# Attention scores from unpadded queries on quarters of the array, and another loading order at the start

## The chip, the cores and the metric

The kernel runs on one core of a Trainium2 chip. The metric is the device time of one execution, in microseconds (us). The engines are named as in the profile: PE is the matmul engine (TensorE) and PEld its weight loads, DVE is VectorE, ACT is ScalarE, POOL is GpSimd, and SP is the engine on which all the DMAs of this kernel are issued. They run side by side and wait for one another at semaphores; each takes its instructions in the order in which they stand.

## What is computed

Attention of 4 batches, 8 heads, 576 positions and head dimension 64, and then two feed-forward layers on the 2304 rows that come out:

```python
mask_local = (rel >= 0) & (rel < 32)                    # heads 0 to 3
mask_strided = (rel >= 0) & (pos_k % 32 == pos_q % 32)  # heads 4 to 7
x = softmax(where(mask, q @ k.T / 8, -1e9)) @ v         # then (2304, 512)
h = x @ w_in;  x = (h - tanh(h)) @ w_out                # d_ff = 2048
xn = x / sqrt(mean(x * x) + 1e-6) * rms_g
x = (silu(xn @ w_gate) * (xn @ w_val)) @ w_out          # d_ff = 1536
```

Activations are float32 and the weights float64. The kernel decodes the float64 words of a weight tile to a high and a low float32r part on ACT and DVE, and every product of the two layers is three matmuls (high by high, low by high, high by low).

## The kernel before

**Blocks and groups.** The rows are cut into nine blocks of 256: blocks 0 to 3 are the first 256 positions of the four batches, block 4 the last 64 positions of all four, blocks 5 to 8 the middle 256 positions. `groups = [(0, 1), (2, 3), (4,), (5, 6), (7, 8)]` pass through the first layer one after the other; the second layer follows on 512 rows at a time. In the first layer a unit `(g, f, a, e)` is group g, slice f of 16 of d_ff, and rows a to e: twelve matmuls `ps_h<-xs,w`, then tanh and a split on ACT and DVE, then twelve matmuls `ps_x<-g,w`. `xs` holds the attention output of the group, split into two parts.

**Attention of a block.** `Local` does heads 0 to 3 and `Dense` heads 4 to 7 (block 4 has `Strided` for these, on POOL and DVE). Each has two parts of three stages. `st_s` makes scores: `ps_s` on PE, then four fused mask-and-minimum reductions on DVE (`sm`, `nm`), four exponentials on ACT, and a division on DVE. `st_p` transposes `sm` on PE (`ps_p`) and copies it to `pT`. `st_v` multiplies by v (`ps_v`, tile `v` for Local and `vd` for Dense), and ACT (L353, L446) and DVE (L354, L447) write the two halves of the result to `xs`. So a block has four score stages, except block 4, which has two.

**Scores before.** The queries of two heads stand in one tile, `qz` or `qd`, that is padded with zeros off the diagonal, so that one matmul over all 128 rows and 128 columns of the array gives the scores of two heads: a stage is four such matmuls of 64, 96 or 128 columns (64 keys for Dense in blocks 0 to 3, 128 in blocks 5 to 8). The zeros come from memsets, and the queries from DMAs of 64 partitions, in pieces of 256 bytes. Each matmul of float32 shows as two in the trace, so a stage of four shows as x8. The stage takes one PSUM tile of the pool `ps_m` (block 0 takes `ps_m` and `ps_h` in turn), and each of these pools has two.

**What sets the order.** A string `START` writes out the beginning, letter by letter: `a` to `e` and `A` to `E` load blocks 0 and 1, `t` the table of masks, `w` a weight, `0` and `1` run the next stage of a block, `s` decodes one step, `U` runs a unit. Then a loop goes through the units; `st1.to` decodes weights ahead of it, and `pe_work` hands out the attention stages of the next group over the f. A scheduler then orders the instructions of each engine from the program's priorities and its own estimates of time; it may take a matmul from a later stage into an earlier place. A DMA on SP waits for the eighth one before it. Weights (`raw`, 512 KB) and the attention tiles of blocks 0 and 1 share the 32 buffers of pool `wts`.

```python
START = 'dt0AB0w00100ss100w1CDsbEU101w10csw1a1sw110w0Usw1s1e'
```

Of the kernel before, what the change touches and what calls it, by code (L numbers as in the profile page):

```python
# [17 lines left out]
BIG = 1.0e30  # L18
# [3 lines left out]
START = 'dt0AB0w00100ss100w1CDsbEU101w10csw1a1sw110w0Usw1s1e'  # L22
# [3 lines left out]
def attn_moe_moe_kernel(  # L26
# [54 lines left out]
    PR = 4 * 64  # L81
# [16 lines left out]
    tab = one.tile([128, 416], F32, name="tab")  # L98
    mask, ident = tab[:, 0:96], tab[:, 160:288]
    dmask = {64: tab[:, 96:160], 128: tab[:, 288:416]}  # L100
    qz = one.tile([128, 4, 2, 128], F32, name="qz")
# [108 lines left out]
    def copy(j, i):  # L210
        if j < EA and "aavaaaaa"[4 * j + i] == "v":
            return nc.vector.tensor_copy
        return nc.scalar.copy


    class Local:
# [9 lines left out]
        def load_qk(self):  # L226
            if self.j < EA:
                self.kT = wts.tile([128, 1024], F32, tag="w", name="kT")[:, :2 * self.kw]
                self.kT = self.kT.rearrange("r (p t) -> r p t", p=2)
                self.qz = wts.tile([128, 1024], F32, tag="w", name="qz").rearrange("r (u p t) -> r u p t", p=2, t=128)  # L230
                (nc.vector if self.j == 0 else nc.gpsimd).memset(self.qz[0:64, :, :, 64:128], 0.0)
                nc.gpsimd.memset(self.qz[64:128, :, :, 0:64], 0.0)
            else:
                self.kT = one.tile([128, 2, 4 * (W + 64)], F32, tag="kT", name="kT")[:, :, :self.kw]
                self.qz = qz
                if self.j == EA:
                    nc.gpsimd.memset(qz, 0.0)
            for b, t0, n, x0 in self.runs:
                for hh in range(2):
                    r = slice(64 * hh, 64 * hh + 64)  # L240
                    nc.sync.dma_start(  # L241
                        out=self.qz[r, x0 // 64:(x0 + n) // 64, :, r].rearrange("r u p t -> r (u p) t"),
                        in_=q_loc[b, r, t0 // 32:(t0 + n) // 32, :],
                    )
                o = self.at[x0 // 64]
                d = W if t0 == 0 else 0
                nc.sync.dma_start(out=self.kT[:, :, o + d:o + W + n], in_=k_loc[b, :, :, t0 - W + d:t0 + n])

        def load_v(self, i):
            us = list(self.units[i])  # L250
            self.v[i] = room(self.j, att, "v", tag="v")[0:96, :512].rearrange("k (u f) -> k u f", u=2)
            if self.wide(us[0]) == 64:
# [757 lines left out]
```

## Time and profile before

| what | us |
|---|---|
| median of 3 runs (lowest 945.73, highest 947.6) | 946.35 |
| the profiled execution | 946.1 |
| its span, from the first to the last instruction | 944.3 |
| PE busy in that span | 927.7 |
| DVE / ACT / POOL busy | 510.5 / 357.9 / 65.2 |

The profile is one execution, and its times count from the start of the span. PE is the engine to follow. A busy PE is not a PE at its peak: matmuls overlap, and each is recorded for longer than the next one has to wait, so the price of a group of matmuls is read as the distance from its start to the start of the next group. The granted clock (PEclk) is a share of 2.4 GHz.

### The profile page before, as it was taken

The numbers are of one execution on the slowest core, as the hardware profiler recorded it, in microseconds if no ns is written. First come the engines' busy times: TensorE is split into PE (matmuls) and PEld (weight loads), VectorE is DVE, ScalarE is ACT, GpSimd is POOL, SyncE is SP. The second block draws the span as 40 slices with busy tenths as digits, with TensorE's granted clock in tenths as the row PEclk, the third lists the DMA queues.
The fourth block names the chain that finished last, engine by engine and source line by source line (L and its number), as shares of the span: only waits on it lengthen the run. The fifth ranks groups of instructions, "written<-read, shape, count | busy, mean of one in ns | idle before, by whom it ended". The sixth has DMA issues, their size and how long they took to land.

```text
span 944.3 us, 13675 instructions
## 1 busy us (share of the span) xinstructions
PE 927.7 (98%) x5274; PEld 782.9 (83%) x5274; DVE 510.5 (54%) x1223; ACT 357.9 (38%) x838; POOL 65.2 (7%) x105
## 2 busy tenths in 40 slices
PE   6899999999999999999999999999999999999998
PEld 5788888888999888888888888888888888888897
DVE  4899998883554434249999783262125312421212
ACT  5776753322554443246656332222112211111211
POOL 2000035760000000000000000000000000000000
PEclk9799999999999999999999999999999999999999
DMA  9936334420321300065535201101010001000100
GB/s 210 336 123 216 117 84 133 110 81 1 111 68 62 89 32 1 1 220 180 162 113 196 76 37 44 45 1 45 1 44 1 23 1 45 0 1 1 45 1 23
DMA packets 51488, 72.66 MB, mean 77 GB/s; under 512 B 24928, under 2 KB 35552, under 8 KB 51424
## 3 DMA queue, kind: packets, MB, share of 16 engines
q1 hardware_dynamic: 51424, 71.80, 24.6%
q8 instruction: 41, 0.67, 0.3%
q14 instruction: 23, 0.19, 0.1%
HBM read 62.34 MB, written 9.44 MB: 76 GB/s over the span
## 4 chain that ended last, share of the span: by engine, by line
PE 94%; DVE 2%; DMA 1%; SPq 1%; issue 0%; ACT 0%
PE ps_x L111 37%; PE ps_h L111 37%; PE ps_m L111 16%; PE ps_s L111 2%; PE ps_v L111 2%; DMA raw<-in_w_in_dram 1%; PE ps_p L326 1%; PE ps_p L426 1%; DVE ct L142 0%; DVE ct L139 0%; SPq L241 0%; DVE w L151 0%; SPq L379 0%; DVE ct L138 0%; DVE sm L297 0%
## 5 line engine op out<-in xcount | busy, mean ns | idle before, releaser
L111 PE MATMUL ps_x<-g,w 128*128 128x512 f32 (+1 forms) x984 | 220.9, 368 | 0.0
L111 PE MATMUL ps_h<-xs,w 128*128 128x512 f32 (+1 forms) x984 | 220.2, 368 | 0.2 <-DVE tg L653 0.2
L111 PEld LDWEIGHTS ps_h<-xs,w 128*128 128x128 f32 x984 | 170.4, 191 | 29.2 <-DVE xs L354 0.4
L111 PEld LDWEIGHTS ps_x<-g,w 128*128 128x128 f32 x984 | 168.7, 188 | 29.5
L111 PE MATMUL ps_h<-xn,w 128*128 128x512 f32 (+1 forms) x720 | 159.0, 369 | 0.0
L111 PE MATMUL ps_m<-xn,w 128*128 128x512 f32 (+1 forms) x720 | 158.6, 368 | 0.0
L111 PE MATMUL ps_x<-w,p 128*128 128x512 f32 x648 | 157.9, 391 | 0.0
L765 DVE SCALAR_TENSOR_TENSOR s<-ps_m,s 128x512 f32<-128x512 f32 (+1 forms) x60 | 38.2, 637 | 219.1 <-PE ps_m L111 219.1
L111 PEld LDWEIGHTS ps_h<-xn,w 128*128 128x128 f32 x720 | 126.8, 188 | 24.4
L111 PEld LDWEIGHTS ps_m<-xn,w 128*128 128x128 f32 x720 | 126.0, 188 | 23.1
L111 PEld LDWEIGHTS ps_x<-w,p 128*128 128x128 f32 x648 | 120.7, 188 | 25.6
L653 DVE SCALAR_TENSOR_TENSOR tg<-ps_h,tg 128x512 f32<-128x512 f32 (+1 forms) x82 | 51.0, 622 | 87.5 <-ACT tg L648 87.5
L764 ACT ACTIVATE s<-ps_h 128x512 f32<-128x512 f32 (+1 forms) x60 | 33.3, 556 | 159.4 <-PE ps_h L111 159.4
L648 ACT ACTIVATE tg<-ps_h 128x512 f32<-128x512 f32 (+1 forms) x82 | 44.5, 543 | 99.9 <-PE ps_h L111 96.5
L767 ACT CAST p<-s 128x512 fp32r<-128x512 f32 (+1 forms) x60 | 34.7, 578 | 121.1 <-DVE s L765 121.1
L659 ACT CAST g<-tg 128x512 fp32r<-128x512 f32 (+1 forms) x82 | 46.6, 569 | 49.5 <-DVE tg L653 49.3
L664 DVE TENSOR_TENSOR g<-tg,g 128x512 fp32r<-128x512 f32 (+1 forms) x82 | 53.4, 651 | 17.0 <-ACT g L659 16.6
L131 ACT ACTIVATE ca<-raw 128x512 f32<-128x512 f32 x68 | 45.7, 674 | 42.4 <-DVE ct L139 18.6
L768 DVE TENSOR_TENSOR p<-s,p 128x512 fp32r<-128x512 f32 (+1 forms) x60 | 38.2, 637 | 25.1 <-ACT p L767 24.9
L150 ACT CAST w<-ct 128x512 fp32r<-128x512 f32 x68 | 42.0, 620 | 16.8 <-DVE ct L142 16.7
L151 DVE TENSOR_TENSOR w<-ct,w 128x512 fp32r<-128x512 f32 x68 | 46.5, 689 | 3.0 <-ACT w L150 2.8
L139 DVE SCALAR_TENSOR_TENSOR ct<-ca,ct 128x512 uint32<-128x512 uint32 x68 | 46.6, 689 | 0.2
(87 smaller groups left out, 681.2 us busy)
## 6 DMA issues: line engine op xcount, KB each, us to landing
raw<-in_w_out_dram SPq DMA_DIRECT2D x28, 512.0 KB, 5.5
raw<-in_w_in_dram SPq DMA_DIRECT2D x16, 512.0 KB, 7.9
raw<-in_w_gate_dram SPq DMA_DIRECT2D x12, 512.0 KB, 3.7
raw<-in_w_val_dram SPq DMA_DIRECT2D x12, 512.0 KB, 3.7
x2d<-xe SPq DMA_DIRECT2D x36, 128.0 KB, 1.8
x<-x2d SPq DMA_DIRECT2D x16, 256.0 KB, 4.0
out_dram<-o SPq DMA_DIRECT2D x16, 256.0 KB, 2.0
v<-in_v_loc_dram SPq DMA_DIRECT2D x14, 192.0 KB, 2.6
```

The costliest lines, as they stand in the source:

```text
L111: nc.tensor.matmul(out_, lhsT, rhs, start=start, stop=stop, skip_group_check=True)
L131: nc.scalar.mul(out=a, in_=hi.bitcast(F32), mul=2.0 ** -111)
L139: nc.vector.scalar_tensor_tensor(out=t, in0=a, scalar=0x80000000, in1=t, op0=ALU.bitwise_and, op1=ALU.bitwise_or)
L150: nc.scalar.copy(out=t[:, 0], in_=self.b)
L151: lo_eng.tensor_tensor(out=t[:, 1], in0=self.b, in1=t[:, 0].bitcast(F32), op=ALU.subtract)
L648: nc.scalar.activation(out=t, in_=h_of[g, f, a], func=ACTF.Tanh, scale=WS)
L653: nc.vector.scalar_tensor_tensor(out=t, in0=h_of.pop((g, f, a)), scalar=WS, in1=t, op0=ALU.mult, op1=ALU.subtract)
L659: nc.scalar.copy(out=t[:, 0], in_=t_of[g, f, a])
L664: nc.vector.tensor_tensor(out=t[:, 1], in0=t_of.pop((g, f, a)), in1=t[:, 0].bitcast(F32), op=ALU.subtract)
L765: nc.vector.scalar_tensor_tensor(out=s, in0=r[1], scalar=WS, in1=s, op0=ALU.mult, op1=ALU.mult)
L767: nc.scalar.copy(out=t[:, 0], in_=s)
L768: nc.vector.tensor_tensor(out=t[:, 1], in0=s, in1=t[:, 0].bitcast(F32), op=ALU.subtract)
```

## The change

**Scores.** The padded tiles and their memsets go; `ql` and `qd` hold the queries of two heads on 64 partitions each, loaded by one DMA in pieces of 2 KB. A stage is now eight matmuls of 64 rows by 64 columns of the array: head half `hh` picks the rows, and which of the two units of 64 queries picks the columns. The two `hh` write two PSUM tiles of the same pool. The softmax code is shared (`softmax`), and the first 64 positions are computed at full width with a mask of their own.

**Heads in natural order.** Dense multiplies by v with eight matmuls of 64 columns where it had sixteen of 32. The end of `Strided` (`fin`) moves its result across partitions with four matmuls by the identity (`ps_o`) in place of a DVE transpose. `PR` grows from 256 to 384 words, so POOL and DVE do the products of `Strided` in fewer, larger pieces. The inputs k and v are padded by 32 positions outside the kernel, which makes each load of v and of the local keys one DMA.

**Order.** `START` now loads the table and all of block 0, then most of block 1, then two weights, and runs all of block 0 before anything of block 1. The first layer decodes three slices ahead instead of four (`f + 3`), and the attention stages of the next group end one f sooner (`rem - 1`). The copy of one transposed tile in block 0 goes from DVE to ACT.

```diff
-START = 'dt0AB0w00100ss100w1CDsbEU101w10csw1a1sw110w0Usw1s1e'
+START = 'tabcdeABCwwDE00000000s0000sU1111s1111wsU1111'
-    PR = 4 * 64
+    PR = 6 * 64
...
-        if j < EA and "aavaaaaa"[4 * j + i] == "v":
+        if j < EA and "aaaaaaaa"[4 * j + i] == "v":
...
+            for b, t0, n, x0 in self.runs:
+                nc.sync.dma_start(
+                    out=self.q[:, x0 // 64:(x0 + n) // 64].rearrange("r u p t -> r (u p) t"),
+                    in_=q_loc[b, :, t0 // 32:(t0 + n) // 32, :],
+                )
...
-            for u in us:
-                for p in range(2):
-                    w = self.wide(u)
-                    mm(
-                        ps[:, u - us[0], p, :w], self.qz[:, u, p, :],
-                        self.kT[:, p, self.at[u] + 96 - w:self.at[u] + 96], True, True,
-                    )
+            ps = [
+                ps_pool.tile([128, 512], F32, tag=ps_tag, name="ps_s")[:, :192].rearrange("q (p t) -> q p t", p=2)
+                for _ in range(2)
+            ]
+            for p in range(2):
+                for k, u in enumerate(us):
+                    for hh in range(2):
+                        r = slice(64 * hh, 64 * hh + 64)
+                        mm(
+                            ps[hh][64 * k:64 * k + 64, p, :], self.q[r, u, p, :],
+                            self.kT[r, p, self.at[u]:self.at[u] + 96], True, True,
+                        )
...
-                    t = prod(gn * 2, W)
-                    nc.vector.transpose(
-                        out=t.rearrange("p (c j) r -> p c j r", j=2),
-                        in_=self.o[:, 0:gn, :].rearrange("l c (j d) -> l c j d", d=32),
-                    )
+                    lanes = ident.rearrange("k (p h l) -> k h p l", p=2, h=2)
+                    for c in range(gn):
+                        for hh in range(2):
+                            mm(ps[64 * hh:64 * hh + 64, :, c, :], self.o[:, c, :], lanes[:, hh], True, True)
...
-            st1.to(2 * (f + 4))
+            st1.to(2 * (f + 3))
...
-                wk.run_pe(max(rem, 1))
+                wk.run_pe(max(rem - 1, 1))
```

SP at the start of the program before: block 0's queries (`qz`, `qd`) come as two DMAs each, and the first weight (`raw`) stands behind them.

```order
L259 DMA v<-in_v_loc_dram 96x2x256
L801 DMA tab<-in_tabs_dram 128x416
L241 DMA qz<-in_q_loc_dram 64x8x64 x2
L247 DMA kT<-in_k_loc_dram 128x2x256
L379 DMA qd<-in_q_den_dram 64x8x64 x2
L383 DMA kd<-in_k_den_dram 128x512
L253 DMA v<-in_v_loc_dram 64x256
L259 DMA v<-in_v_loc_dram 96x256
L388 DMA vd<-in_v_den_dram 64x1024
L241 DMA qz<-in_q_loc_dram 64x8x64 x3
L247 DMA kT<-in_k_loc_dram 128x2x256
```

The same place of the changed program, from the loads of block 1 on: two weights follow each other, and all loads of block 2 (the third `ql`) stand ahead of the third weight.

```order
L256 DMA ql<-in_q_loc_dram 128x512
L261 DMA kT<-in_k_loc_dram 128x2x288
L347 DMA qd<-in_q_den_dram 128x512
L349 DMA kd<-in_k_den_dram 128x512
L269 DMA v<-in_v_loc_dram 96x2x256
L123 DMA raw<-in_w_in_dram 128x512 x2
L269 DMA v<-in_v_loc_dram 96x2x256
L354 DMA vd<-in_v_den_dram 64x1024
L256 DMA ql<-in_q_loc_dram 128x512
```

In the program before, the first weight is the 19th DMA and the second the 27th; in the changed one they are the 14th and 15th, and the third is the 25th.

ACT of the changed program behind the last exponentials of block 0: the first decoding step of the first three weights (`ca<-raw`) stands among block 0's copies.

```order
L224 ACTIVATE sm,ss<-sm,nm 128x64
L130 ACTIVATE ca<-raw 128x512
L224 ACTIVATE sm,ss<-sm,nm 128x64 x3
L306 COPY pT<-ps_p 96x512
L130 ACTIVATE ca<-raw 128x512
L385 COPY pT<-ps_p 64x512
L306 COPY pT<-ps_p 96x512
L327 CAST xs<-ps_v 128x2x128
L385 COPY pT<-ps_p 64x512
L149 CAST w<-ct 128x512
L405 CAST xs<-ps_v 128x2x16x8
```

Behind these rows come the last two casts of block 0 with the third `ca<-raw` between them, so what is left of block 0 on ACT stands behind the landing of that weight.

PE in the first layer of blocks 5 and 6 before: a score stage is one piece of four matmuls among those of the layer.

```order
L111 MATMUL ps_h<-xs,w 128x256 x7
L111 MATMUL ps_x<-g,w 128x256 x11
L111 MATMUL ps_s<-kT,qz 128x96 x4
L111 MATMUL ps_x<-g,w 128x256
L111 MATMUL ps_h<-xs,w 128x256
L111 MATMUL ps_s<-kd,qd 128x128 x4
L111 MATMUL ps_h<-xs,w 128x256 x11
```

The same place of the changed program: each stage is two pieces of four quarter matmuls, the first of one `hh` and the second of the other, with matmuls of the layer between them.

```order
L110 MATMUL ps_v<-pT,vd 64x64 x8
L110 MATMUL ps_s<-kT,ql 64x96 x4
L110 MATMUL ps_x<-g,w 128x256
L110 MATMUL ps_h<-xs,w 128x256 x12
L110 MATMUL ps_x<-g,w 128x256 x11
L110 MATMUL ps_s<-kT,ql 64x96 x4
L110 MATMUL ps_s<-kd,qd 64x128 x4
L110 MATMUL ps_x<-g,w 128x256
L110 MATMUL ps_h<-xs,w 128x256 x12
L110 MATMUL ps_x<-g,w 128x256 x7
L110 MATMUL ps_s<-kd,qd 64x128 x4
```

What moved is that a stage is split at its two PSUM tiles, and each second piece waits for DVE to have emptied the buffer that it takes.

## Rows read from the trace of the kernel before

**Rows 1.** Windows of the span: busy us (instructions) by engine, PEclk, DMA share, GB/s.

```profile
20.00:30.00 10.00, 7.35 (x113) 5.98 (x113) 7.78 (x33) 6.68 (x26) 0.00 (x0) 0.68 1.07 293
30.00:40.00 10.00, 8.79 (x50) 8.30 (x51) 7.63 (x27) 7.05 (x23) 0.00 (x0) 0.64 1.05 277
53.00:153.00 100.00, 100.00 (x663) 82.85 (x664) 94.75 (x253) 64.16 (x164) 15.28 (x22) 1.00 0.39 117
153.00:240.00 87.00, 87.00 (x436) 72.39 (x435) 61.34 (x160) 27.06 (x68) 40.88 (x63) 1.00 0.26 74
```

**Rows 2.** All waits of PE from 53 us to the end of the span.

```profile
PE ps_h L111 <- DVE tg L653: 0.2, 1, 0.2
```

**Rows 3.** The chain that ended last, 12 to 27 us: start, us, what.

```profile
12.24 7.22 DMA raw<-in_w_in_dram
19.48 6.64 DMA raw<-in_w_in_dram
26.14 0.67 ACT ca L131
```

**Rows 4.** Timeline of PE in the first 54 us: start, us, instructions [idle before].

```profile
7.24 3.70 PE L111 MATMUL ps_s<-kT,qz 128*128 128x64 f32 x16 [7.24 <-DMA kT<-in_k_loc_dram]
...
32.87 3.55 PE L111 MATMUL ps_h<-xs,w 128*128 128x256 f32 x13
...
47.06 1.92 PE L111 MATMUL ps_h<-xs,w 128*128 128x256 f32 x10
...
53.00 1.69 PE L111 MATMUL ps_h<-xs,w 128*128 128x256 f32 x12 [0.18 <-DVE tg L653]
```

**Rows 5.** Groups of ACT, 0 to 50 us: line, tiles, count, busy and mean, idle before.

```profile
L131 ACT ACTIVATE ca<-raw 128x512 f32<-128x512 f32 x9 | 6.0, 670 | 5.1 <-DMA raw<-in_w_in_dram 3.9 <-DVE ct L139 1.3
L409 ACT ACTIVATE sm<-sm,nm 128x64 f32<-128x64 f32 x16 | 5.4, 335 | 3.7 <-DVE nm L403 3.7
L150 ACT CAST w<-ct 128x512 fp32r<-128x512 f32 x7 | 4.4, 625 | 0.7 <-DVE ct L142 0.7
L305 ACT ACTIVATE sm<-sm,nm 128x96 f32<-128x96 f32 x12 | 4.3, 360 | 0.0
L446 ACT CAST xs<-ps_v 128x256 fp32r<-128x256 f32 x4 | 2.5, 615 | 1.4 <-PE ps_v L111 1.4
L428 ACT COPY pT<-ps_p 64x512 f32<-64x512 f32 x4 | 2.3, 575 | 0.4 <-PE ps_p L426 0.4
```

**Rows 6.** Timeline of ACT: block 1's last result cast.

```profile
45.83 0.63 ACT L446 CAST xs<-ps_v 128x256 fp32r<-128x256 f32 x1
```

**Rows 7.** DMA packets, 2 to 12 us (queries, keys), then 41 to 47 us (weights alone).

```profile
DMA packets 4433, 2.19 MB, mean 219 GB/s; under 512 B 3527, under 2 KB 4241, under 8 KB 4433
DMA packets 667, 2.45 MB, mean 408 GB/s; under 512 B 73, under 2 KB 73, under 8 KB 666
```

**Rows 8.** Timeline of PE among blocks 5 and 6.

```profile
234.40 1.02 PE L111 MATMUL ps_s<-kT,qz 128*128 128x96 f32 x8
235.27 1.08 PE L111 MATMUL ps_s<-kd,qd 128*128 128x128 f32 x8
236.10 2.98 PE L111 MATMUL ps_x<-g,w 128*128 128x512 f32 x12
...
245.53 0.69 PE L111 MATMUL ps_v<-pT,v 96*64 96x64 f32 x16
246.15 1.09 PE L111 MATMUL ps_x<-g,w 128*128 128x256 f32 x7
247.17 0.69 PE L111 MATMUL ps_v<-pT,vd 128*32 128x64 f32 x32
247.79 0.86 PE L111 MATMUL ps_x<-g,w 128*128 128x256 f32 x5
248.49 1.60 PE L111 MATMUL ps_h<-xs,w 128*128 128x256 f32 x12
249.92 1.02 PE L111 MATMUL ps_s<-kT,qz 128*128 128x96 f32 x8
```

More of the change, by code (lines that the diff above doesn't have):

```diff
@@ L96, in attn_moe_moe_kernel @@
     one = poolT.enter_context(tc.tile_pool(name="one", bufs=1, side="right"))
[L98 to L101, printed above, removed]
+    tab = one.tile([128, 512], F32, name="tab")
+    mask, mask0, ident = tab[:, 0:96], tab[:, 96:192], tab[:, 384:512]
+    dmask = {64: tab[:, 192:256], 128: tab[:, 256:384]}
     sc = {}
@@ L227, in load_qk @@
             if self.j < EA:
[L228 to L232, printed above, removed]
-            else:
[L234 to L237, printed above, removed]
+                q = wts.tile([128, 1024], F32, tag="w", name="ql")
@@ L238, in load_qk @@
+                kT = wts.tile([128, 1024], F32, tag="w", name="kT")
+            else:
+                q = one.tile([128, 512], F32, tag="ql", name="ql")
+                kT = one.tile([128, 8 * (W + 64)], F32, tag="kT", name="kT")
+            self.q = q[:, :512].rearrange("r (u p t) -> r u p t", p=2, t=64)
+            self.kT = kT[:, :2 * self.kw].rearrange("r (p t) -> r p t", p=2)
             for b, t0, n, x0 in self.runs:
[L239 to L243, printed above, removed]
-                    )
+                nc.sync.dma_start(
+                    out=self.q[:, x0 // 64:(x0 + n) // 64].rearrange("r u p t -> r (u p) t"),
+                    in_=q_loc[b, :, t0 // 32:(t0 + n) // 32, :],
+                )
@@ L322, in st_p @@
             sm = self.sm.pop(i)
-            for u in range(nu):
+            for hh in range(2):
                 for p in range(2):
-                    w = self.wide(self.units[i][u])
-                    nc.tensor.transpose(ps[:w, u, p, :], sm[:, u, p, :w], ident)
-            pT = room(self.j, att, "pT", tag="pT")[0:96, :512].rearrange("k (u p t) -> k u p t", u=2, p=2)
-            for a, e, w in self.parts(i):
-                copy(self.j, 2 * i)(out=pT[:w, a:e], in_=ps[:w, a:e])
+                    nc.tensor.transpose(ps[:, hh, p, :], sm[:, hh, p, :], ident)
@@ L330, in st_p @@
+            pT = room(self.j, att, "pT", tag="pT")[0:96, :512].rearrange("k (h p t) -> k h p t", h=2, p=2)
+            copy(self.j, 2 * i)(out=pT, in_=ps)
             self.pT[i] = pT
@@ L337, in st_v @@
             pT, v = self.pT.pop(i), self.v.pop(i)
-            for u in range(nu):
+            for u in range(2):
                 for p in range(2):
@@ L970, in lay_out @@
     r2 = row % 64
+    first = near & ((row >= 64) | (col >= 32))
     same = (r2 // 8 == c2 // 8) & (c2 <= r2)
```

194 lines of the change are left out of this document (76 added, 118 removed).

## The prediction

> **What bounds the kernel now.** I read the windows first, then what PE waited for, then the chain of the first 27 us, then PE's own rows. From 53 us to the end PE is the bound: it waited 0.2 us in all that time [rows 2], although DVE was busy 94.75 us of the 100 from 53 to 153 us [rows 1]. So after 53 us the time is the sum of PE's pieces, and it ends as much earlier as PE reaches its steady stretch earlier, plus what its pieces gain or lose. Before 53 us it is otherwise: PE waits 7.24 us for the first keys, the first layer's first matmul starts at 32.87, and only from 47.06 does it run on with both blocks of group 0 finished [rows 4]. The chain there runs through two weights, landing at 19.46 and 26.12 us, and ACT's decoding behind them [rows 3]; the granted clock is 0.68 and 0.64 from 20 to 40 us [rows 1]. Two terms decide, then: the start, and the price of the score pieces behind it.
>
> **The start.** The bytes ahead of the first weight stay about as they were (3.6 MB with it), but the pieces change: nine DMAs of queries in 256-byte pieces (4608 packets) become four in 2 KB pieces (512 packets). The price of a packet comes from two stretches in which the 16 DMA engines were full [rows 7]: 16 x 10 us / 4433 = 36 ns at a mean of 494 bytes, 16 x 6 us / 667 = 144 ns at 3.7 KB. A line between them gives 28 ns for 256 bytes, 54 for 1 KB, 89 for 2 KB and 158 for 4 KB. Before, the 19 DMAs up to the first weight cost 238 us of engine time, 14.9 us on 16 engines; in the new order the 14 cost 170, or 10.7 us. That is 4.2 us earlier: the first weight lands near 15.2 us instead of 19.5, the second follows at 16.5 instead of 26.1. The third, behind all of block 2's loads, costs another 120 us of engine time, and lands near 24. The first keys come 1.6 us earlier, near 5.7. The bounds for the first weight are 19.5 (no gain) and 11 us (all at the 408 GB/s of the weights alone).
>
> What that is worth is set by ACT, the busiest chain here. In the new order ACT has, up to block 1's last cast to `xs`, 32 exponentials, 8 copies of transposed tiles, 7 first decoding steps, 3 weight casts, 8 casts to `xs` and 4 instructions of the first units. With the means of [rows 5] (0.36 or 0.335, 0.575, 0.67, 0.625, at most 0.615, some 0.37 us) that is 28.7 us at most, and about 25 from start to start, since each overlaps the next by some 0.06 us. It begins near 7.6 us, some 2 us behind the first keys. Two waits come in, because the order puts the decoding of the first and third weight in front of what is left of block 0: 13 exponentials end near 12.2 and the first weight lands at 15.2 (3 us); block 0's copies end near 21.5 and the third weight lands at 24 (2.5 us). With 3 us for waits on DVE and PE (3.7 and 2.1 us of such waits in [rows 5]) this gives 7.6 + 25 + 5.5 + 3 = 41 us. Before, that cast ended at 46.46 [rows 6]. **Gain 5.4 us**; between 2, if the half clock keeps PE slow until 44 us, and 8, if ACT's waits shrink.
>
> Decoding less far ahead, and the copy of one tile that moves from DVE to ACT (0.6 us), lie beside this: by 41 us two weight casts fewer have been made than before at 46.46. Behind that point DVE's work up to a given unit is no larger than before, so PE should remain the bound, as in [rows 2]; if that cover is gone, a missing weight costs PE its decoding, some 3 us once. The memsets on POOL and the fewer DMAs on SP delay nobody later. `Strided` with larger pieces, and its transposes, which leave DVE, are off PE's path too: DVE is busy 61 of 87 us while they run, from 153 to 240 us [rows 1].
>
> **The score pieces behind the start.** A stage of four full-array matmuls takes 0.87 us (234.40 to 235.27) or 0.83 (235.27 to 236.10) [rows 8]. I counted the pieces in the order of both programs, from the point that stands at 53 us before. There are 24 stages: 24 x 0.83 = 19.9 us. Afterwards they are 49 groups of four quarter matmuls, since the order splits almost every stage at its two PSUM tiles (one group that stood ahead of that point falls behind it): 7 groups of 64 columns, 26 of 96, 16 of 128. No row shows a quarter score. The nearest is `ps_v`, two column halves in turn, 64 columns: eight in 0.62 us (245.53 to 246.15) [rows 8], so 0.31 for four. If the columns don't matter, 49 groups cost 15.2 us; if time grows with the columns (0.47 and 0.62), 24.3. In the full-array stages 96 and 128 columns cost the same, so I stay near the lower end, with 0.34 and 0.43: 17.9 us, a gain of 2.0.
>
> A group that stands alone pays for coming and going. Between two `ps_v` pieces seven `ps_x` of 256 columns take 1.02 us (246.15 to 247.17), where twelve `ps_h` of that size take 1.43 (248.49 to 249.92), 0.12 each: 0.18 too much. Five after a piece take 0.70, 0.10 too much [rows 8]. So leaving costs 0.10 and entering a column-tiled piece 0.08; a full-array score piece pays no entry (`ps_h` and then `ps_s`, 248.49 to 249.92, is 1.43 as said). Entries rise from 26 to 59: +2.7. Pieces among the first layer's matmuls rise from 64 to 74: +1.0. The 16 `ps_o` matmuls cost 16 x 0.0775 = 1.2; Dense's eight matmuls of 64 columns cost the 0.62 of sixteen of 32 (247.17 to 247.79) [rows 8]. **The sum is -2.0 + 2.7 + 1.0 + 1.2 = +2.9 us**, between +0.2 and +9.3.
>
> The Trainium skill, in "TensorE: Matmul & The Clock Gate", section LDWEIGHTS, says that a weight load takes its columns over 1.2 ns whatever its rows. By it eight quarter matmuls (16 loads of 64 columns, 0.85 us) save nothing against four full ones (8 loads of 128), the 49 groups cost 20.9 us, and the kernel would take 947.0 instead of 944.0. The 16 loads of a `ps_v` piece in 0.62 us, 39 ns each, are less than its 53, so I stay with the row.
>
> **Sum.** The profiled execution took 946.1 us, 0.25 below the median. 946.1 - 5.4 + 2.9 = 943.6; against the median, 943.9, so I say 944.0.
>
> **Rivals.** *Quarters overlap.* If the second half of a stage ran under the first, on the other 64 rows, 24 groups would vanish from the sum: -24 x 0.36 = -8.7, 935 us. For it: the first two stages of block 0 do have their four quarters in turn. Against it: after those the order lets one row half go first and the other later, most often with matmuls of the layer between them. The Trainium skill, in "TensorEngine Tiling (Array Packing)", section Key Properties, says that different tiles load and multiply in parallel; no run here shows row halves doing so.
>
> *PE waits for PSUM (slower).* A stage needs both buffers of `ps_m`, so each of some 40 second or later groups waits until DVE has read the tile that stood there, and behind that wait the whole queue of PE stands. DVE's two reads take some 0.3 us and can lie behind others of 0.6. At 0.2 us each that is +8, 952 us; at 0.05 (+2) the gain of the sum is gone, and from 0.1 (+4) the kernel is slower by 0.2%. For it: DVE is nearly full until 153 us [rows 1]. Against: the scores before also wait for DVE's readers and PE lost 0.2 us by all of it [rows 2], and the scheduler puts work in between.
>
> *The start gives little.* ACT stands in front of two weights with block 0's copies behind it, and PE, on small pieces, stays at the half clock that rows 1 show for 20 to 40 us, longer than I think. With 2 us of gain the time is 947.3: no difference.
>
> *The sum holds*: 944.0, between 941 and 947.
>
> **How the numbers follow.** The sum holds 0.48 (0.27 faster, 0.20 same, 0.01 slower), quarters overlap 0.08, PE waits for PSUM 0.22, the start gives little 0.22 (0.15 same, 0.07 slower). About 0.2%, 1.9 us, is what a measurement of this kernel tells from no change. So faster 0.35, same 0.35, slower 0.30. The range runs from 938, part of the way to the overlap, to 951, most of the way to the waits for PSUM; it leaves out some 0.07 on either side, and takes in the upper bound of the pieces (946.1 - 5.4 + 9.3 = 950).
>
> **What would show it.** In the profile of the changed kernel: the first `ca<-raw` of ACT near 15 us and the third near 24, each behind a wait for DMA; block 1's last cast near 41; the first matmul of the first layer between 21 and 26. Among blocks 5 to 8, four quarter scores of 96 columns from start to start in 0.31 to 0.35 us, with 0.1 more before and behind. PE's waits behind 50 us should stay under 1 us; several us there for `ps_s` on DVE mean the second rival. The sum is wrong if the first layer reaches its steady stretch later than 44 us, or if a group of four costs 0.45 us or more.

## The result, and the profile after

The changed kernel is slower. Its median over 4 runs is 958.63 us (956.62 to 960.6), that of the kernel before, measured beside it, 946.04 us (945.38 to 947.6): a ratio of 1.0131, with a 95% interval of 1.0105 to 1.0156. The forecast was 944.0 in a range of 938 to 951. The profiled execution took 956.62 us, with a span of 954.8; against the 946.1 us of the profile before that is 10.5 us more.

To see where they come from I set the two traces side by side at equal work: in each I count the matmuls of the two feed-forward layers that PE has done, at 0.12 us for 256 columns and 0.24 for 512, and compare the times at which the same amount is reached. At 5 us of layer work, which is where block 1's result is in `xs` and the first layer runs on, the changed kernel stands at 47.90 us and the kernel before at 46.12: **+1.8 us, where the forecast had -5.4**. From there to 320 us of work another **8.7 us** are lost, **where the forecast had 2.9**, and from 320 us of work to the end the distance stays at 10.5. So both terms of the sum failed, and by similar amounts: 7.2 and 5.8 us.

The windows of the changed kernel (columns as in [rows 1]; the last stretch lies in the first layer of block 4 and then of blocks 5 and 6, while the scores of blocks 5 to 8 are made):

```profile
20.00:30.00 10.00, 7.50 (x75) 5.85 (x73) 4.28 (x10) 3.77 (x7) 0.00 (x0) 1.00 1.06 329
30.00:40.00 10.00, 7.37 (x66) 6.41 (x67) 8.13 (x49) 8.73 (x39) 0.00 (x0) 1.00 1.03 409
53.00:153.00 100.00, 98.84 (x664) 78.51 (x661) 89.05 (x228) 62.80 (x156) 4.29 (x5) 1.00 0.33 104
153.00:240.00 87.00, 86.86 (x452) 69.81 (x451) 61.49 (x135) 26.73 (x62) 42.58 (x48) 1.00 0.27 82
240.00:330.00 90.00, 90.00 (x820) 79.38 (x819) 41.99 (x162) 44.60 (x143) 0.00 (x0) 1.00 0.24 71
```

Between 20 and 30 us ACT is busy for 3.77 us, against 6.68 before [rows 1], and DVE for 4.28, against 7.78: the two engines that the start hangs on stand still. The 1.00 for PEclk in the first two lines is no record of a full clock (last section). The two orders of PE ahead of the prediction lie in that last stretch too: they are said to be from the first layer of blocks 5 and 6, but show that of block 4, with the scores of 5 and 6 in it. Behind 53 us PE is the bound again, as before; it is idle for 1.2 us up to 153 and for 0.1 in the 177 us behind. The 8.7 us are therefore not waits, but mostly PE's own work.

The waits of PE over the whole span (engine, tile and line, what released it: us in total, times, longest), the five largest:

```profile
PE ps_s L110 <- DMA kT<-in_k_loc_dram: 6.2, 1, 6.2
PE ps_v L110 <- ACT pT L306: 4.1, 2, 4.0
PE ps_s L110 <- DVE nm L218: 2.6, 3, 1.9
PE ps_h L110 <- ACT xs L405: 1.9, 1, 1.9
PE ps_h L110 <- DVE xs L328: 1.1, 1, 1.1
```

The first is the wait for the first keys, 1.0 us shorter than the 7.24 of [rows 4]; the forecast had said 1.6. The second and the fourth are ACT's doing. The timeline of ACT shows why (start, us, instruction, [idle before, and what ended it]):

```profile
15.94 0.66 ACT L130 ACTIVATE ca<-raw 128x512 f32<-128x512 f32 x1 [3.81 <-DMA raw<-in_w_in_dram]
16.50 0.33 ACT L224 ACTIVATE sm<-sm,nm 128x64 f32<-128x64 f32 x1
...
17.50 0.56 ACT L306 COPY pT<-ps_p 96x512 f32<-96x512 f32 x1
...
27.58 0.66 ACT L130 ACTIVATE ca<-raw 128x512 f32<-128x512 f32 x1 [4.51 <-DMA raw<-in_w_out_dram]
28.14 0.59 ACT L405 CAST xs<-ps_v 128x256 fp32r<-128x256 f32 x1
...
47.38 0.63 ACT L405 CAST xs<-ps_v 128x256 fp32r<-128x256 f32 x1
```

ACT stands for 3.81 us in front of the first weight, with three exponentials of block 0 and all its copies to `pT` queued behind; PE, which needs the first `pT`, stands for 4.0 us with it. Then ACT stands for 4.51 us in front of the third weight, with the last cast of block 0 behind it, and the exponentials of block 1 behind that, from 30.14 us on. Block 1's last cast ends at 48.01 us, not at 41.

The place among blocks 5 to 8 that answers to [rows 8], in the timeline of PE (a group of four quarter matmuls shows as x8):

```profile
257.63 0.52 PE L110 MATMUL ps_h<-xs,w 128*128 128x256 f32 x3
258.08 0.55 PE L110 MATMUL ps_s<-kT,ql 64*64 64x96 f32 x8
258.56 0.86 PE L110 MATMUL ps_h<-xs,w 128*128 128x256 f32 x5
259.35 0.55 PE L110 MATMUL ps_s<-kT,ql 64*64 64x96 f32 x8
259.82 0.74 PE L110 MATMUL ps_h<-xs,w 128*128 128x256 f32 x4
260.40 1.24 PE L110 MATMUL ps_x<-g,w 128*128 128x256 f32 x9
```

From 257.63 to 260.40 are 2.77 us. They hold one stage of 96 columns, in two groups, and twelve `ps_h` that take 1.43 us undisturbed [rows 8]. The stage therefore costs 1.34 us, 0.67 a group: 0.48 from the group's start to the next instruction's, and 0.19 for coming and going. A full-array stage before cost 0.83 to 0.87 [rows 8], 0.90 with its way out by the same reckoning. The forecast had put a group of 96 columns at 0.34 and 0.18.

### The profile page after: what moved, and what is told of

It is laid out like the page before. It is cut to its first block, busy times and chain, and to the rows that moved or that the text cites. A ratio compares the mean times of both kernels' runs of the same rounds, so it can differ in the third digit from the quotient of the medians.

```text
span 954.8 us, 13658 instructions
## 1 busy us (share of the span) xinstructions
PE 931.6 (98%) x5322; PEld 769.4 (81%) x5322; DVE 506.6 (53%) x1185; ACT 360.6 (38%) x835; POOL 47.2 (5%) x57
## 3 DMA queue, kind: packets, MB, share of 16 engines
q1 hardware_dynamic: 36320, 72.11, 23.6%
## 4 chain that ended last, share of the span: by engine, by line
PE 80%; DVE 1%; issue 0%; POOL 0%
PE ps_x L110 31%; PE ps_h L110 30%; PE ps_m L110 16%; PE ps_s L110 1%; PE ps_v L110 1%; DVE so L483 0%; PE ps_p L304 0%; PE ps_p L383 0%; POOL pr L476 0%; PE ps_o L110 0%; DVE g L623 0%; DVE os L749 0%; DVE tg L612 0%
## 5 line engine op out<-in xcount | busy, mean ns | idle before, releaser
L110 PE MATMUL ps_h<-xs,w 128*128 128x512 f32 (+1 forms) x984 | 225.2, 372 | 3.7 <-ACT xs L405 1.9
L224 ACT ACTIVATE sm<-sm,nm 128x96 f32<-128x96 f32 (+2 forms) x136 | 49.9, 368 | 32.7 <-DVE nm L218 32.5
L149 ACT CAST w<-ct 128x512 fp32r<-128x512 f32 x68 | 41.9, 622 | 18.5 <-DVE ct L141 18.5
```

What stands on the lines that cost most here:

```text
L110: nc.tensor.matmul(out_, lhsT, rhs, start=start, stop=stop, skip_group_check=True)
L149: nc.scalar.copy(out=t[:, 0], in_=self.b)
L224: nc.scalar.activation(out=sm[:, hh, p], in_=sm[:, hh, p], func=ACTF.Exp, scale=-1.0, bias=nm[:, hh, p:p + 1], accum_out=ss[:, hh, p:p + 1],)
```

## The experiments

All but four edits are made on the changed kernel. The theory for the start is that the order of ACT's instructions, decoding in front of block 0's copies, turned the landings of two weights into waits of everything else; the rivals are the loading order itself, and the half rate that PE has at the start (last section). The theory for the rest is that a quarter group has a price of its own, paid twice where a stage is split; the rivals are a late PSUM buffer, decoding that is not far enough ahead, and `ps_o`. `behind(x, y)` is an edge that has the scheduler place x after y and adds no wait of its own. Each ratio is to the kernel before, run beside it.

### The start

**The old START in the changed kernel (startb).** If the new order of the start is what costs, the old order should give it back.

```diff
-START = 'tabcdeABCwwDE00000000s0000sU1111s1111wsU1111'
+START = 'dt0AB0w00100ss100w1CDsbEU101w10csw1a1sw110w0Usw1s1e'
```

> The changed kernel with the START string of the kernel before; all else as changed. In the changed kernel block 1's attention and 5.0 us of first-layer matmuls were done at 47.90 us, before at 46.12, so the new order gained nothing there (-5.4 forecast). Theory A, the new order itself costs the time: with the old order and the lighter loads this point comes at 46 us or earlier, and the time falls by 2 to 5 us, to 953 to 956 (from a median of 958.6). Rival B, the order is harmless and the small matmuls of blocks 0 and 1 are slower: the point stays near 48 and the time within 1 us of 958.6.

Measured: 959.01 us, ratio 1.0139 (1.0124 to 1.0154), no gain; at 5 us of layer work it stands 3.1 us behind the kernel before. ACT's timeline shows the same fault with another weight, the second, which landed only then:

```profile
28.98 0.66 ACT L130 ACTIVATE ca<-raw 128x512 f32<-128x512 f32 x1 [4.38 <-DMA raw<-in_w_in_dram]
```

So the string alone is not the cause. What both have in common is a decoding step that stands on ACT in front of a landing, with other work behind it.

**The new START in the kernel before (before_start).** The counterpart: the loading order alone, with the padded queries.

> The kernel before with the START string of the change alone (queries still padded and loaded in 256-byte pieces, full-array scores). Theory A1, the order puts the decoding of weights that land late ahead of attention work on ACT, and the heavier loads land later still: no gain, 0 to 4 us slower, 946 to 950. Rival, the order gains by itself what was forecast and the quarters lose it: 941 to 944.

Measured: 954.76 us, 1.01 (1.0083 to 1.0118). It loses 8.2 us up to 5 us of layer work and 0.4 behind that. ACT stands there 4.85 us for the first weight and 4.57 for the third, as in the changed kernel, and PE waits for the zeros in `qd`, which POOL now writes too late (PE's waits):

```profile
PE ps_s L111 <- POOL qd L376: 6.8, 1, 6.8
```

The unpadded queries are needed for the new order, and the waits on ACT come with the order whatever the queries.

**Two more weights before block 2 (w4).** With `ABCwwwwDE` in place of `ABCwwDE` the third weight no longer stands behind block 2's loads.

> The changed kernel with two more weights loaded right behind the first two, so ahead of block 2's loads (START with wwww for ww). Theory A1, ACT stood 4.5 us before the third first-decoding step because that weight landed at 27.6 us, and block 1's exponentials stood behind it: the third weight now lands near 20, the wait shrinks below 1.5 us, block 1's last cast comes near 45 instead of 48, and the time falls by 2 to 4 us, to 954 to 957. Rival A2, the length of block 0's and block 1's chain, run one after the other at the half clock, sets the start: the wait goes, the cast stays near 48 and the time within 1 us of 958.6.

Measured: 959.5 us, 1.0161 (1.0116 to 1.0206), and +2.2 at 5 us of layer work. The third weight landed at 18.5 us, but ACT then stood 4.72 us for the first and 2.92 for the fifth (at 30.06), and PE waited 5.9 us for exponentials. The wait moved to another weight, so this run doesn't decide what the waits cost.

**Another order on ACT alone (act_order, act_order2).** The loads stay as they are; only the place of the first decoding steps on ACT changes. In act_order the first weight's goes behind block 0's exponentials and the third's behind block 1's:

```diff
+    for c, e in ((0, 15), (2, 31)):
+        behind(cas[c], exps[e])
```

> The changed kernel with ACT's order alone moved: the first decoding step of weight 1 stands behind block 0's sixteen exponentials, that of weight 3 behind block 1's. Theory A1, weights that land late (15.9 and 27.5 us) with attention work behind them in ACT's queue cost the start its gain: ACT's 4.5 us wait goes, block 1's last cast comes at 43 to 46 us in place of 48.0, and the time falls by 2 to 4 us from 958.6, to 954.5 to 956.5. Rival A2, the chain of block 0 and then block 1 is as long anyway: the cast stays within 1 us of 48 and the time within 1 us.

Measured: 955.28 us, 1.0099 (1.0084 to 1.0115). At 5 us of layer work it stands 0.1 us ahead of the kernel before, 1.9 better than the changed kernel. But ACT still stands 3.85 us for the first weight and 1.83 for the second, and block 0's copies stand behind these. So act_order2 puts the first one behind block 0's fourth copy, and the second behind its second cast to `xs`:

```diff
+    for c, l, e in ((0, cps, 3), (1, cts, 1), (2, exps, 31)):
+        behind(cas[c], l[e])
```

> The changed kernel with ACT's order moved further: the first decoding step of weight 1 behind block 0's four copies, that of weight 2 behind its second cast, that of weight 3 behind block 1's exponentials. In the run before, ACT still stood 3.9 and 1.8 us for weights 1 and 2 (landed at 17.7 and 20.6 us) with block 0's copies behind them. Theory A1: these stalls go, block 1's last cast comes at 41 to 44 us, and the time falls by 1.5 to 4 us more, to 951.5 to 954. Rival A3, the first layer cannot start before weight 1 is decoded, near 24 us, and block 1's chain follows it at the half clock: within 1 us of 955.3.

Measured: 951.66 us, 1.0063 (1.0048 to 1.0078). By the medians that is 7.0 us less than the changed kernel, by the ratios 6.4. ACT's timeline:

```profile
17.07 0.66 ACT L138 ACTIVATE ca<-raw 128x512 f32<-128x512 f32 x1
...
18.91 0.69 ACT L138 ACTIVATE ca<-raw 128x512 f32<-128x512 f32 x1 [0.65 <-DMA raw<-in_w_in_dram]
...
31.54 0.65 ACT L138 ACTIVATE ca<-raw 128x512 f32<-128x512 f32 x1
...
41.29 0.64 ACT L413 CAST xs<-ps_v 128x256 fp32r<-128x256 f32 x1
```

The waits for weights are down to 0.65 us, although all three landed later than in the changed kernel: at 16.63, 18.89 and 30.00 us, where it has 15.91, 17.62 and 27.50. Block 1's last cast ends at 41.93 instead of 48.01, and at 5 us of layer work the kernel stands 4.3 us ahead of the kernel before: the gain of the start is there, and a fixed queue behind two landings had hidden it. Nothing but these three edges was edited, and the loads came no earlier, so these waits, with all that stood behind them, cost the 7.0 us: this is shown. What of it is the waits alone isn't: PE, too, reached its full rate earlier, at 34.0 us instead of 40.4 (last section). Between the two traces the gain is 6.1 us at 5 us of layer work and 4.3 at the end: a fall of the clock behind that (last section) takes 1.9 of it back, and the changed kernel's profiled execution was the fastest of its four.

### The score pieces

**Quarters in the kernel before (before_quarters).** Only blocks 4 to 8, only the scores: the padded tile is kept, each head half reads its own quarter of it, and a stage takes two PSUM tiles, as in the changed kernel.

```diff
+                    for hh in (0, 1):
+                        r = slice(64 * hh, 64 * hh + 64)
+                        todo.append((
+                            hh, ps[hh][64 * k:64 * k + 64, p, :], self.qz[r, u, p, r],
+                            self.kT[r, p, self.at[u]:self.at[u] + 96],
+                        ))
+            for hh, out_, lhsT, rhs in todo:
+                mm(out_, lhsT, rhs, True, True)
```

> The kernel before with one part of the change alone: the scores of blocks 4 to 8 as eight quarter matmuls in two PSUM tiles of ps_m (the queries still lie in the padded tiles; the quarters read their diagonal). Theory C, as read from the trace of the changed kernel: a group of four of 96 columns costs 0.68 us with its way out, a full-array stage 0.90, and where the two groups stand apart the stage costs 1.07 on the mean: 18 stages, +3 to +5 us, 949 to 951. Rival I, the loss behind the start is from elsewhere (the transposes by PE, the pace, blocks 0 to 3): 945 to 947.

Measured: 950.22 us, 1.0045 (1.0031 to 1.0058). That is 4.05 us more, at 18 stages. Two groups of a stage in PE's timeline:

```profile
252.73 0.55 PE L111 MATMUL ps_s<-kT,qz 64*64 64x96 f32 x8
253.21 0.74 PE L111 MATMUL ps_h<-xs,w 128*128 128x256 f32 x4
...
254.60 0.65 PE L111 MATMUL ps_s<-kd,qd 64*64 64x128 f32 x8
255.18 0.98 PE L111 MATMUL ps_x<-g,w 128*128 128x256 f32 x6
```

The price of 0.48 for 96 columns and 0.58 for 128 belongs to the quarters, then, and not to unpadded tiles or another neighbourhood.

**The same with the stage kept together (before_pairs).** The matmuls of the two row halves alternate, the second half first, and an edge holds each behind the one before. A mark, a small write of DVE to each PSUM tile, can only come when the tile is free, and the first matmul is placed behind both marks:

```diff
+        mark = [nc.vector.memset(ps[hh][0:1, 0, 0:1], 0.0) for hh in range(2)]
+        last = None
+        for hh, out_, lhsT, rhs in quarters:
+            i = mm(out_, lhsT, rhs, True, True)
+            if last is None:
+                behind(i, mark[0])
+                behind(i, mark[1])
+            else:
+                behind(i, last)
+            last = i
```

> The kernel before with the scores of blocks 4 to 8 as quarters, but all eight of a stage kept together, row halves in turn (two one-element writes by DVE to the two PSUM tiles go first, the first matmul follows them). Theory C: 0.69 us for a stage in place of 0.90, 18 stages, -3 to -4.5 us, 941 to 943. Rival D, the wait for both PSUM tiles is paid by PE: 945 or above.

Measured over 11 runs: 944.73 us, 0.9983 (0.9974 to 0.9992). Now the stage is one record of sixteen:

```profile
254.56 0.56 PE L111 MATMUL ps_s<-kT,qz 64*64 64x96 f32 x16
255.05 0.51 PE L111 MATMUL ps_x<-g,w 128*128 128x256 f32 x2
...
258.60 0.67 PE L111 MATMUL ps_s<-kd,qd 64*64 64x128 f32 x16
259.20 1.46 PE L111 MATMUL ps_h<-xs,w 128*128 128x256 f32 x10
```

Eight quarter matmuls take 0.49 us from start to start, where four took 0.48; with 128 columns 0.60 and 0.58. The second row half runs wholly under the first. What the split costs is the second group: 950.22 - 944.73 = 5.5 us over 18 stages, 0.30 each. Two lone groups of 96 columns, 1.34 us, against one whole stage, 0.49 + 0.19, would be 0.66 a stage; it is less because some groups of before_quarters ran beside one of another stage.

The forecast for this run, 941 to 943, was missed all the same. At 0.68 us a stage against 0.90, 18 stages would save 4.0 us; measured are 1.4 against the kernel before (946.17 beside it). By equal work the trace gains 1.8 us among blocks 5 to 8, where 16 of the stages lie. One new wait of PE for DVE takes 0.5; the rest isn't assigned.

**The stage kept together in the changed kernel (pair).**

> The changed kernel with the eight quarter matmuls of a stage kept together, the two row halves in turn: two one-element writes by DVE to the two PSUM tiles come first, and the first matmul follows both of them. Theory C, row halves run side by side: a whole stage costs 0.69 us with the way out (0.58 and 0.11), where the 26 stages behind the start now cost 1.07 on the mean, so the time falls by some 8 to 10 us, to 949 to 951. Rival D, the wait for both PSUM tiles eats it: PE waits several us for DVE, or the later stages push others, and the time stays at 955 or above.

Measured: 957.79 us, 1.0128 (1.0113 to 1.0143): no difference from the changed kernel that these runs can tell. Between 170 and 320 us of layer work, among blocks 5 to 8, it gains 2.2 us on the kernel before where the changed kernel loses 3.9. At the start it loses 6.0 more than the changed kernel. The edges hold for blocks 0 and 1 too, where PE now waits for a mark and for DVE's reductions (PE's waits):

```profile
PE ps_p L405 <- DVE nm L236: 5.7, 1, 5.7
...
PE ps_s L110 <- DVE ps_s L119: 2.3, 1, 2.3
```

And the granted clock falls at 153 us (last section). So pairs pay where PE has other work to do, and cost where it has none.

**The second tile from another pool (two_pools).** If a late PSUM buffer is what splits the stages, a buffer of `ps_h` for the second tile should join them:

```diff
-                ps_pool.tile([128, 512], F32, tag=ps_tag, name="ps_s")[:, :2 * nk].rearrange("q (p t) -> q p t", p=2)
-                for _ in range(2)
+                pl.tile([128, 512], F32, tag=tg, name="ps_s")[:, :2 * nk].rearrange("q (p t) -> q p t", p=2)
+                for pl, tg in ((ps_m, "m"), (ps_h, "h"))
```

> The changed kernel with the PSUM tile of the second row half taken from ps_h instead of ps_m. Theory G, a stage that holds both buffers of ps_m holds up the stages behind it, so block 3's last results come only at the end of group 0 and PE waits 1.3 us there: that wait goes, the heads 0 to 3 stage of blocks 5 to 8 runs as one piece of eight, and the time falls by 3 to 5 us, to 953.5 to 955.5. Rival H, ps_h is what the first layer's units take in turn, so they wait instead: PE waits of several us for ps_h, time at 957 or above.

Measured: 957.11 us, 1.0116 (1.0102 to 1.013). Stages are still split in part, and PE's wait of 1.1 us behind 53 us became one of 0.5; at 5 us of layer work it stands 2.1 us behind the changed kernel, because ACT now waits 6.87 us for the third weight. The time is the one that the rival expected, but the long waits for `ps_h` that it named are not there. A buffer of its own for the second tile is not enough to keep a stage together.

### The end of group 0, and `ps_o`

**Decoding four slices ahead again (f4).** The changed kernel's one late wait is 1.1 us of PE for block 3's `xs`, at the end of group 0.

```diff
-            st1.to(2 * (f + 3))
+            st1.to(2 * (f + 4))
...
-                wk.run_pe(max(rem - 1, 1))
+                wk.run_pe(max(rem, 1))
```

> The changed kernel with the old pace: decoding four slices ahead (f + 4) and the attention of the next group spread over rem instead of rem - 1. PE waits 1.3 us at 149 us for the last results of block 3 in the changed kernel. Theory E, the new pace brings that wait: it goes, and the time falls by 1 to 2 us. Rival F, the old pace pushes the last stages even later: the wait stays or grows, and the time is within 1 us or higher.

Measured: 960.42 us, 1.0162 (1.013 to 1.0195). The wait stays at 1.1 us. The spread of the runs (958.18 to 964.71) overlaps the changed kernel's. So decoding less ahead and ending the attention stages sooner are not the cause of that wait, and no cost that these runs can tell; the forecast's zero for it held.

**The old way out of `Strided` and Dense's v (order2_oldtail).** act_order2 with the DVE transpose in place of the `ps_o` matmuls, and v in 32 columns as before.

> The changed kernel with ACT's order of act_order2 and, besides, the old way of Strided's end and of the tail heads: DVE transposes in place of the four ps_o pieces. Theory K, the ps_o pieces cost PE what their rows show, 4 x 0.56 = 2.2 us, not the 1.2 forecast: 951.7 - 2.2 = 949.5, between 948.5 and 950.5. Rival L, the transposes put DVE behind at the end of group 0 and PE waits there longer: 951 or above. The run named combined differs from this one by the pairs in blocks 4 to 8 alone (940.9).

Measured over 10 runs: 949.25 us, 1.0034 (1.0024 to 1.0043), 2.4 less than act_order2. In the changed kernel `ps_o` is four pieces of four matmuls, and each must come and go (its PE):

```profile
172.86 0.45 PE L110 MATMUL ps_o<-tab,so 128*64 128x64 f32 x8
173.24 0.72 PE L110 MATMUL ps_h<-xs,w 128*128 128x512 f32 x2
```

0.38 from start to start, 0.56 with both ends. By equal work the two pieces that stand alone cost 0.6 each; the other two share an end with another small piece, so four make about 2.2 us. The forecast had 1.2, the matmuls without their ends. The 2.4 need not be `ps_o` alone: in this trace PE's wait at the end of group 0 is 0.7 us where act_order2 has 1.4, and the fall of the clock behind it is absent.

### Together

**combined** is order2_oldtail with the stages of blocks 4 to 8 kept together, and those of blocks 0 to 3 free.

> The changed kernel with ACT's order of the run above, the quarters of blocks 4 to 8 kept together in pairs of row halves, and the old way of Strided's end and of the tail heads (DVE transposes in place of the four ps_o pieces, which cost 0.56 us each in the trace of the changed kernel). Sum from the traces: start 1 to 3 us earlier than the kernel before, blocks 2 and 3 +0.2, the wait at the end of group 0 +1.3, blocks 4 to 8 -2 to -3: 942 to 945. Rival, the stages of blocks 2 and 3 and the pairs are late at the end of each group and PE waits more there: 946 or above.

Measured over 6 runs: 940.94 us, 0.9951 (0.9939 to 0.9963). This beats both kernels. The steps of medians are 958.6, then 951.7 with ACT's order, 949.3 with the old way out, 940.9 with whole stages. The last step is 8.3 us by the medians and 6.3 by the traces, 5.8 of them among blocks 5 to 8, as between before_quarters and before_pairs. PE's largest wait in its trace that is left behind the first keys:

```profile
PE ps_h L110 <- ACT w L173: 3.8, 1, 3.8
```

**combined_w** moves the first weight's load ahead of block 1's, to take that wait away.

```diff
-START = 'tabcdeABCwwDE00000000s0000sU1111s1111wsU1111'
+START = 'tabcdewABCwDE00000000s0000sU1111s1111wsU1111'
```

> The kernel named combined with the first weight loaded ahead of block 1 (START begins tabcdewABCw). In combined PE waited 3.8 us for the first weight, which landed at 18.8 us. Theory A1, with ACT's order mended the landing of weight 1 is what is late next at the start: it lands near 13, the wait shrinks below 2 us, and the time falls by 1 to 2 us from 940.9, to 939 to 940. Rival, block 1's keys and queries then land later and its scores start later: 940.5 or above.

The wait shrank to 1.1 us. In the profiled execution it stands 4.8 us ahead of the kernel before at 5 us of layer work, where combined stands 2.3 ahead. But the median is 941.2 us over 5 runs, 0.9948 (0.9934 to 0.9961), the same as combined. The profiled execution of combined was the slowest of its six, 942.89, so the difference of the two traces is at least partly one between executions; a gain of this move isn't shown.

**before_best** keeps the old START and the old kernel, has before_pairs' stages, and puts the decoding steps of the second and third weight behind other work on ACT.

> The kernel before with the pairs of quarters in blocks 4 to 8 and ACT's order moved: the first decoding step of weight 2 behind eight of block 1's exponentials, that of weight 3 behind block 0's last casts. ACT stood 2.5 us for weight 2 before. Theory A1 holds for the kernel before too: 1 to 2.5 us less than with the pairs alone (944.7), 942 to 943.7. Rival, PE at the half clock and not ACT sets the start before: 944 to 945.5.

Measured over 12 runs: 943.59 us, 0.9974 (0.996 to 0.9988). The order on ACT adds little there: 944.73 to 943.59 lies within the spread of its runs (940.73 to 946.58).

## Why the prediction was wrong, step by step

**The start: the step that failed is the size of ACT's waits and what stands behind them.** The forecast saw that decoding stands in front of block 0's copies, and put 3 and 2.5 us on it. Measured were 3.81 and 4.51. Its chain, 7.6 + 25 + 5.5 + 3 = 41, reads in the trace 7.46 + 27.0 (ACT's work) + 8.3 (two weights) + 5.2 (other waits) = 48.0. So of the 7 us too few, 2.8 are the waits for weights, 2.2 the other waits and 2.0 ACT's work. That the waits for weights, with what stood behind them, ate the gain is shown by act_order2, where they are gone and the cast ends at 41.93. The number 41 itself is no success of the sum: it stood in the forecast with 5.5 us of waits for weights and 3 of others, and came about there with 0.65 and 7.8 (6.73 + 26.8 + 0.65 + 7.8).

Part of the longer waits is the price of DMA packets. The first weight was decoded from 15.94 (forecast near 15), the third from 27.58 (forecast near 24). The profile's count for 2 to 27 us of the changed kernel:

```profile
DMA packets 4210, 7.24 MB, mean 290 GB/s; under 512 B 399, under 2 KB 2319, under 8 KB 4209
```

16 engines x 25 us / 4210 is 95 ns at a mean of 1720 bytes; the forecast's line through [rows 7] gives 78 there. So the same packets took 25 us, not 20.4. By the trace's records of single packets, the 629 of 4 KB took 237 ns each, where the line gives 158: that is 50 of the 89 us of engine time by which these records lie above the line. Those of 1 and 2 KB took 63 and 108 ns, where it gives 54 and 89. The upper end of the line came from weights alone, whose 4 KB packets took 163 ns; among smaller pieces they cost more.

In PE's timeline the first matmul of the first layer came at 24.43, inside the 21 to 26 given; after it PE stood for block 0's last cast, and the steady stretch began at 46.74 us, later than the 44 that the prediction named as its own refutation:

```profile
24.43 1.65 PE L110 MATMUL ps_h<-xs,w 128*128 128x256 f32 x6
...
46.74 2.73 PE L110 MATMUL ps_h<-xs,w 128*128 128x256 f32 x12
```

**The score pieces: the right mechanism, mis-sized.** A group of four was put at 0.34 (96 columns) and 0.43 (128) from `ps_v`; measured 0.48 and 0.58. `ps_v` alternates its two column halves too, with 64 columns; that a score takes longer per column was the upper bound of the forecast (0.47 and 0.62), and the choice of the lower end was the mistake. Coming and going, 0.18, measured 0.19. By equal work the scores cost +5.0 us: +0.2 in blocks 2 and 3, +0.9 in block 4 and +3.9 in blocks 5 to 8, against a forecast of -2.0 + 2.7 + 1.0 = +1.7. That is less than 49 groups at the measured price would give, because two of the 16 stages of blocks 5 to 8 ran whole (from 241.06 and 245.61 us, in 0.50 and 0.60) and some groups found a partner, as in these rows of the changed kernel's PE:

```profile
276.86 0.30 PE L110 MATMUL ps_s<-kT,ql 64*64 64x96 f32 x2
276.88 0.33 PE L110 MATMUL ps_s<-kd,qd 64*64 64x128 f32 x2
...
277.47 1.34 PE L110 MATMUL ps_x<-g,w 128*128 128x256 f32 x9
```

Two groups of different stages, one on each row half, run through each other in 0.61 us.

**The rest of the sum.** `ps_o` took about 2.2 instead of 1.2. The wait at the end of group 0, 1.1 us, had no term. With the scores this makes 8.3 of the 8.7 us behind the start; the remainder isn't assigned. Decoding less ahead at nothing, and POOL and SP delaying nobody, held.

**The rivals.** *Quarters overlap*: its mechanism is real, eight matmuls cost what four cost, but the changed kernel splits most of the pairs, which the prediction had said against it. The Trainium skill's sentence in "TensorEngine Tiling (Array Packing)", section Key Properties, that different tiles load and multiply in parallel, agrees with the 0.49 against 0.48 us of before_pairs and before_quarters. The Trainium skill's rule in "TensorE: Matmul & The Clock Gate", section LDWEIGHTS, gives the sixteen loads of a stage an estimated 0.85 us; a whole stage's 0.49 to 0.60 us speaks against it, as the prediction had said from `ps_v`. The prediction's own price was wrong too. *PE waits for PSUM*: its sign was several us of `ps_s` on DVE behind 50 us, and there are none; its time, 952, was nearest for a wrong reason. *The start gives little*: its mechanism, ACT in front of two weights with block 0's copies behind, is what happened, and more of it than the rival allowed: not a gain of 2 us but a loss of 1.8. PE also stayed at the half rate longer, up to 40.4 us where the kernel before has 37.2. The forecast's bounds for the start ran from a gain of 2 to one of 8 us; they should have gone beyond no gain, because a strict order behind a landing that comes late can lose as well as win.

## What to carry to other kernels

Before a load is moved, look at where its first reader stands on an engine that works in order, and what is queued behind it: an early decoding step in front of a late DMA stops everything behind it, and moving three such steps was worth 7.0 us here, and none of the orders of loads tried gave anything by itself. When a matmul is cut into tiles of the array, keep the tiles that can run beside each other next to each other in the program, and fix that order; with its ends, a stage of quarters that stayed whole cost three quarters of a full-array stage (0.68 against 0.90 us, 96 columns), a split one 1.5 times as much (1.34); of the first, less came through in the time of the kernel than the rows promise (before_pairs). Count pieces as well as matmuls, since each piece on a part of the array cost 0.19 us to enter and leave.

## What was not expected of the hardware

**Two row halves cost what one does.** Eight matmuls on quarters, 64 rows each, 0.49 us; four on one row half, 0.48 (above).

**The clock fell after a wait of PE in the middle of the run.** In act_order2, PE stood for 1.38 us at the end of group 0, and in the window behind it the granted clock is 0.57, a mean that lies near the lower of its levels (1.2 of 2.4 GHz is 0.50). The windows of act_order2:

```profile
142.00:146.00 4.00, 2.62 (x23) 1.67 (x23) 2.02 (x5) 0.96 (x2) 3.10 (x4) 1.00 0.59 186
146.00:150.00 4.00, 4.00 (x17) 3.13 (x17) 2.74 (x10) 0.82 (x4) 2.69 (x3) 0.57 0.15 37
```

PE's timeline there:

```profile
144.69 1.43 PE L110 MATMUL ps_h<-xs,w 128*128 128x512 f32 x5 [1.38 <-DVE xs L336]
...
146.53 4.61 PE L110 MATMUL ps_h<-xs,w 128*128 128x512 f32 x12
```

The same twelve matmuls took 3.04 us in the changed kernel, behind a wait of 1.10 us that no fall of the clock followed (PE's timeline):

```profile
150.50 1.42 PE L110 MATMUL ps_h<-xs,w 128*128 128x512 f32 x5 [1.10 <-DVE xs L328]
...
152.33 3.04 PE L110 MATMUL ps_h<-xs,w 128*128 128x512 f32 x12
```

So the wait cost 1.38 us and some 1.6 more. The traces of startb and pair show such a fall too (0.66 from 152 to 157 us, 0.58 from 152 to 160). The length of the wait alone doesn't tell which: in f4 the clock fell behind a wait of 1.15 us (0.51 from 152.9 to 156.4), and in w4 it stayed at 1.00 behind one of 1.48.

**At the start the profile reads a full clock where it has no record.** The windows above have 1.00 from 20 to 40 us, yet four transposes take 1.09 us at 37.23 and 0.60 at 40.56, and the twelve `ps_h` between them 2.59 us from start to start, where twelve take 1.43 among blocks 5 and 6 before [rows 8]:

```profile
37.23 1.09 PE L304 MATMUL ps_p<-tab,sm 128*96 128x128 f32 x4
37.97 2.76 PE L110 MATMUL ps_h<-xs,w 128*128 128x256 f32 x12
40.56 0.60 PE L383 MATMUL ps_p<-tab,sm 128*64 128x128 f32 x4
```

The trace of the changed kernel has its first record of the clock at 40.4 us, at the full level, and a window without a record reads 1.00. The trace of the kernel before has records from 20.2 us on: 0.50 from 23.6 to 37.2 us, the lower level, and 1.00 behind that. Its four transposes show what a missing record hides:

```profile
17.54 1.06 PE L426 MATMUL ps_p<-tab,sm 128*64 128x128 f32 x4
...
36.22 1.05 PE L326 MATMUL ps_p<-tab,sm 128*64 128x128 f32 x4
...
37.98 0.60 PE L426 MATMUL ps_p<-tab,sm 128*64 128x128 f32 x4
```

The second stands under a record of 0.50, the third under one of 1.00, and the first, without a record, takes as long as the second. So the half rate of the changed kernel up to 40.4 us is read as the lower level, which the record left out; in act_order2 the first record, again at the full level, is at 34.0 us. The rate of a known matmul is the surer sign.

**The start differs from one execution to the next.** before_quarters and before_pairs share their program with the kernel before up to 87 us of layer work, and stand at -0.44 and +1.06 us there. Of a difference at the start, less than about 1 us in one trace says nothing.
